# Ten of the convolution's 36 pieces as TensorE products with diagonal matrices, and a new order of all steps

## The chip, the core and the metric

The kernel runs on one core of one Trainium2 chip. The metric is the device time of one execution in microseconds (us), taken as the median of several runs. The core's engines work side by side, each in the order of its own queue: TensorE (PE in the profile, with its weight loads as PEld), VectorE (DVE), ScalarE (ACT), GpSimd (POOL), and SyncE (SP), which here only issues DMA transfers. PE writes PSUM, eight banks of 512 fp32 numbers in each of 128 partitions. ACT and DVE read PSUM; POOL works on SBUF alone.

## The reference

Attention for 8 batches and 8 heads, 576 positions, 64 numbers to a head, then a gated unit over the 512 channels that the heads make together:

```python
scores = scale * np.matmul(q, k.transpose(0, 1, 3, 2))        # scale 1/8
cum = np.cumsum(np.maximum(s, 0.0), axis=-1)
bias = -(cum[:, :, :, None] - cum[:, :, None, :])
scores = np.where(causal, -1000000000.0, scores + np.minimum(bias, 0.0))
attn = softmax(scores)                                        # over the keys
x = np.matmul(attn, v)                                        # (8, 576, 512) after the heads are joined
for k in range(5):
    gate_pre += conv_w[k] * xp[:, k:k + S, :]                 # xp: x with four rows of zeros ahead
out = (sigmoid(gate_pre) * (x @ w_val)) @ w_out
```

The sum over five taps is a causal convolution along the sequence, each channel with its own five weights. It is the part that the change touches.

## The kernel before

A tile is one batch with one pair of heads, which is also one batch with one chunk of 128 channels: 32 tiles, numbered 4 times the batch plus the pair. For each tile the kernel does these steps. The names are those of the table that sets the order; a name is followed by the tile's number.

- `s0 s1 s2` (PE, L508): scores of keys against queries, three groups of two PSUM banks, the two heads side by side in the two halves of PE's rows. `s4` does the last 64 keys of four tiles at once.
- The causal mask on the diagonal blocks: either `mk` (POOL, L585) sets zeros in the exponentials, or, for tiles that have no `mk`, PE adds a product of two constant matrices to the scores (L521), which makes the masked ones hugely negative.
- `e0 e1 e2` (ACT, L563): the exponential, 128x1024 from PSUM into one of the buffers P. `e4` is that of `s4`.
- `av0 av` (PE, L600): exponentials against V, 15 products of 65 columns for each head. V' (`vp`, POOL, L477) is V times a weight from the cumulated s, with a column of twos that gives the sum of the row. `rec nm` (DVE) normalise to half of x.
- `xt` (PE, L632): five transposes bring x to channels by positions, in a PSUM bank. `xe` copies it to SBUF in bf16 (tile xT, L376: all plain copies have this line).
- The convolution, on DVE, POOL and ACT. The taps are divided by the last one, so that this one is the plain x. `t1` (DVE, L671) makes gp = x + ratio * x one position back. `t2 t3 t4` add the other three. On DVE (L676) each is one multiply-add, which reads x in PSUM. On POOL it is two steps: a product `p2 p3 p4` into a buffer pr (L660; a few of the products are done by ACT, L658) and a sum into gp (L679).
- `th` (ACT, L694): tanh of gp times the last tap.
- `val` (PE, L706): x times w_val, four products for each half of 288 positions. `glu` (DVE, L715): (tanh + 1) times it.
- `out` (PE, L726): four products of 512 columns per 128 rows, from the glu tiles of two batches. `oe` copies the result out of PSUM, `st` (SP) stores it.

Around it `ld_q ld_k ld_t ld_v` load (`ld_t`: the last 64 positions of q and k, the tails), `c_q c_k` cast to bf16, `qt` or `qq` transpose q and k on PE, `tt` does that for the tails in fp32 (L483), `qe te` copy the results to QKT (L376). `wu` (PE, L626) is a product of 512 columns that nobody reads; 32 of them stand where PE would have nothing to do. The four tiles of the last batch, 28 to 31, are done in two parts, 384 and 192 positions (`u` and `f` in place of `s` and `e`, and steps named like `t1.29.1`).

The order is a table, ORDER: one entry for each step, with the engine that does it (T is PE, V DVE, A ACT, G POOL, S SP) and the buffers or PSUM banks that it takes. The program reads the table from front to back and gives each engine its steps in that order, and each engine executes its queue strictly in order, waiting at a step until what it needs is there. So the table decides which engine does a step and what stands behind it. BUFS is the number of buffers of each kind: 3 for P, 4 for gp, 2 for pr.

Of the kernel before, what the change touches and what calls it, by code (L numbers as in the profile page):

```python
# [210 lines left out]
t2.3:V ld_t.3:S th.1:A:1 vp.1.2:G wu.31:T:5 av0.4:T:6+7 av.4:T:6+7 e0.5:A:0 rec.4:V vp.1.1:G av0.6:T:4+5 nm.4:V
av.6:T:4+5 e1.5:A:0 s2.5:T:2+3 rec.6:V cast_wv:G s1.7:T:6+7 nm.6:V e2.5:A:0 ld_q.3:S:3 xt.4:T:0 tt.2:T:1 xe.4:V
th.0:A:2 av0.5:T:2+3 t1.4:V:2 c_q.2:G:1 av.5:T:2+3 te.2:A val.3.0:T:4 th.3:A:3 rec.5:V nm.5:V val.3.1:T:1 e1.7:A:2
val.1.0:T:5 glu.3.0:V p4.4:G:1 ld_v.2.2:S xt.5:T:2 glu.3.1:V val.1.1:T:3 c_k.2:A:2 glu.1.0:V ld_v.2.4:S s2.7:T:6+7
glu.1.1:V t4.4:G qq.2.0:T:1:5 xe.5:V val.0.0:T:3 e2.7:A:2 val.0.1:T:4 vp.1.3:G t2.4:V ld_v.2.1:S qe.2.0:A t1.5:V:1
p2.5:G:0 av0.7:T:6+7 glu.0.0:V p3.5:A:1 ld_v.2.3:S glu.0.1:V val.2.0:T:3 t3.4:V qe.2.1:A t2.5:G av.7:T:6+7
qq.2.1:T:4:2 rec.7:V nm.7:V val.2.1:T:0 qe.2.3:A cast_wo:G glu.2.0:V xt.6:T:5 xt.7:T:1 xe.6:V qe.2.2:A s0.9:T:6+7
glu.2.1:V s1.9:T:2+3 ld_v.2.0:S xe.7:V e0.9:A:1 p4.5:G:0 out.0.2:T:0 t1.6:V:0 t1.7:V:3 e1.9:A:1 out.0.0:T:4 ld_k.5:S:4
t3.5:G t4.6:V oe.0.2:A:0 s1.8:T:6+7 s0.8:T:2+3 oe.0.0:A:1 t3.7:V mk.9:G val.7.0:T:0 e0.8:A:0 ld_k.3:S:0 t2.6:V
out.0.3:T:4 p3.6:G:1 e1.8:A:0 t2.7:V out.0.1:T:2 ld_t.4:S t4.7:V th.4:A:4 t3.6:G val.4.0:T:3 val.7.1:T:7 th.7:A:3  # L220
glu.4.0:V st.0.2:S val.4.1:T:1 oe.0.3:V:2 t4.5:G th.6:A:1 s2.8:T:5+6 glu.7.1:V s4.2.3:T:3+4 e2.8:A:0 glu.7.0:V
val.6.0:T:7 glu.4.1:V vp.2.0:G ld_v.3.2:S val.6.1:T:0 glu.6.0:V e4.2.3:A ld_v.3.3:S oe.0.1:V:3 s0.10:T:5+6 th.5:A:2
s2.9:T:3+4 c_q.3:G:0 glu.6.1:V av0.8:T:1+2 e2.9:A:1 av.8:T:1+2 val.5.0:T:0 e0.10:A:2 rec.8:V nm.8:V s2.10:T:3+4
vp.2.1:G val.5.1:T:7 e2.10:A:2 glu.5.0:V s1.10:T:1+2 glu.5.1:V s0.11:T:5+6 ld_q.5:S:1 e1.10:A:2 vp.2.2:G xt.8:T:0
av0.9:T:3+4 xe.8:V tt.3:T:7 e0.11:A:0 t1.8:V:2 p4.8:G:1 av.9:T:3+4 te.3:A qq.3.0:T:1:2 rec.9:V ld_t.5:S nm.9:V
# [5 lines left out]
nm.11:V s0.14:T:3+4 out.0.5:T:7 e0.14:A:2 st.0.3:S oe.0.4:V:3 t2.9:V s4.3.3:T:5+6 ld_v.4.2:S t3.10:G th.8:A:0
xt.11:T:4 ld_v.4.1:S s0.13:T:2+3 e4.3.3:A xe.11:V s2.13:T:0+1 e0.13:A:0 t1.11:V:1 val.8.0:T:5 vp.3.3:G val.10.0:T:6
glu.8.0:V th.10:A:3 t3.11:V s1.13:T:2+3 st.0.4:S vp.3.1:G val.8.1:T:5 e2.13:A:0 glu.10.0:V t2.11:V val.10.1:T:6
e1.13:A:0 mk.13:G val.9.0:T:0 glu.8.1:V oe.0.5:A:5 glu.10.1:V val.9.1:T:1 mk.14:G t4.11:V th.9:A:4 s2.14:T:2+3
qq.5.0:T:7:6 ld_k.6:S:0 e2.14:A:2 glu.9.0:V c_k.5:G:0 av0.13:T:4+5 qe.5.0:V av.13:T:4+5 qe.5.1:A val.11.0:T:0
ld_v.4.4:S rec.13:V glu.9.1:V th.11:A:1 s1.14:T:2+3 s0.15:T:6+7 vp.3.2:G nm.13:V e1.14:A:2 ld_v.4.0:S val.11.1:T:1
glu.11.0:V xt.13:T:4 st.0.5:S glu.11.1:V mk.12:G e0.15:A:0 s1.15:T:2+3 xe.13:V s2.15:T:0+1 t1.13:V:2 e2.15:A:0
c_q.4:G:1 qq.5.1:T:7:6 t2.13:V out.1.1:T:5 qe.5.2:A qe.5.3:V av0.14:T:0+1 e1.15:A:0 c_k.4:G:2 av.14:T:0+1 out.1.2:T:7
p4.13:A:0 rec.14:V nm.14:V oe.1.1:A:2 qq.4.0:T:6:2 oe.1.2:V:3 t4.13:G qq.4.1:T:5:3 qe.4.1:A qe.4.0:V xt.14:T:7
out.1.0:T:0 vp.3.0:G xe.14:A t3.13:V qe.4.2:A av0.15:T:1+2 t1.14:V:0 av.15:T:1+2 p4.14:G:1 ld_v.5.2:S qe.4.3:A  # L240
# [5 lines left out]
th.14:A:0 s0.18:T:6+7 vp.4.3:G rec.16:V e0.18:A:1 val.12.0:T:0 nm.16:V ld_t.6:S th.12:A:3 glu.14.1:V val.12.1:T:6
mk.18:G glu.14.0:V xt.16:T:7 th.13:A:4 oe.1.3:V:4 ld_q.7:S:4 val.15.0:T:3 vp.4.2:G xe.16:A glu.12.1:V s1.18:T:4+5
glu.12.0:V s2.18:T:1+2 e1.18:A:1 val.13.0:T:6 glu.15.0:V st.1.0:S t1.16:V:3 vp.5.2:G val.13.1:T:0 e2.18:A:1 st.0.8:S
s0.19:T:3+4 glu.13.0:V t4.16:V ld_k.7:S:2 s4.5.3:T:5+6 e0.19:A:2 av.18:T:1+2 glu.13.1:V c_q.6:G:1 av0.18:T:1+2 t3.16:V
e4.5.3:A s1.19:T:3+4 rec.18:V s2.19:T:5+6 e1.19:A:2 nm.18:V ld_t.7:S out.1.4:T:0 vp.5.3:G t2.16:V e2.19:A:2 xt.18:T:1  # L250
# [593 lines left out]
```

## Time and profile before

| | |
|---|---|
| timed runs (us) | 188.28, 189.47, 189.51; median 189.47 |
| the profiled execution: its span (us) | 188.0 |
| PE busy (us) | 171.6 (91%), 2724 products |
| DVE busy (us) | 166.1 (88%), 322 instructions |
| ACT busy (us) | 169.2 (90%), 229 instructions |
| POOL busy (us) | 163.7 (87%), 147 instructions |
| granted PE clock, mean | 0.986 |

The profile gives the profiled execution from its first to its last instruction, 188.0 us; the page has no other time of it. That is 0.3 us below the fastest and 1.5 us below the median of the timed runs. Durations of single instructions, as the groups give them, include the time in which an instruction's end runs beside the start of the next one; so a group's busy time divided by its count is what one of them adds to the engine's busy time. For PE the ends are modelled, and what a product really takes of PE is read from one start to the next.

### The profile page before, as it was taken

The numbers are of one execution on the slowest core, as the hardware profiler recorded it, in microseconds if no ns is written. First come the engines' busy times: TensorE is split into PE (matmuls) and PEld (weight loads), VectorE is DVE, ScalarE is ACT, GpSimd is POOL, SyncE is SP. The second block draws the span as 40 slices with busy tenths as digits, with TensorE's granted clock in tenths as the row PEclk, the third lists the DMA queues.
The fourth block names the chain that finished last, engine by engine and source line by source line (L and its number), as shares of the span: only waits on it lengthen the run. The fifth ranks groups of instructions, "written<-read, shape, count | busy, mean of one in ns | idle before, by whom it ended". The sixth has DMA issues, their size and how long they took to land.

```text
span 188.0 us, 6658 instructions
## 1 busy us (share of the span) xinstructions
PE 171.6 (91%) x2724; PEld 113.4 (60%) x2724; DVE 166.1 (88%) x322; ACT 169.2 (90%) x229; POOL 163.7 (87%) x147
## 2 busy tenths in 40 slices
...
GB/s 173 272 279 258 244 222 262 346 386 333 185 251 347 168 307 178 334 331 271 169 257 238 328 389 247 205 307 221 62 59 167 3 2 59 223 5 112 43 202 158
DMA packets 62283, 40.46 MB, mean 215 GB/s; under 512 B 47333, under 2 KB 49381, under 8 KB 62250
## 3 DMA queue, kind: packets, MB, share of 16 engines
...
## 4 chain that ended last, share of the span: by engine, by line
PE 39%; ACT 27%; DVE 17%; issue 7%; DMA 6%; SPq 1%; POOL 1%; ACTq 0%; DVEq 0%
ACT P L563 18%; PE bank L706 11%; PE bank L726 9%; PE bank L600 7%; PE bank L508 6%; ACT QKT L376 4%; DVE gp L676 4%; DMA out_dram<-ot 4%; DVE gp L671 3%; DMA gp<-in_s_dram 3%; ACT th L694 2%; DVE xn L619 2%; PE bank L632 2%; DVE glu L715 2%; PE bank L626 2%
## 5 line engine op out<-in xcount | busy, mean ns | idle before, releaser
L563 ACT ACTIVATE P<-bank 128x1024 bf16<-128x1024 f32 x84 | 83.0, 1046 | 4.2 <-PE bank L508 3.4
L676 DVE SCALAR_TENSOR_TENSOR gp<-bank,cwr,gp 128x573 f32<-128x573 bf16 (+5 forms) x72 | 52.7, 744 | 0.9
L679 POOL TENSOR_TENSOR gp<-gp,pr 128x572 f32<-128x572 f32 (+6 forms) x36 | 45.0, 1255 | 6.6 <-DVE gp L676 4.2
L508 PE MATMUL bank<-QKT 64*128 64x128 bf16 (+4 forms) x592 | 37.4, 238 | 5.0 <-DVE QKT L376 1.8
L477 POOL TENSOR_TENSOR Vp<-vst,w 128x650 bf16<-128x650 f32 x32 | 40.6, 1283 | 1.5 <-DMA qkf<-in_k_dram 1.0
L706 PE MATMUL bank<-xT,wv 128*128 128x288 bf16 (+2 forms) x256 | 37.9, 287 | 1.2 <-ACT P L563 0.4
L600 PE MATMUL bank<-Vp,P 128*128 128x65 bf16 x960 | 35.6, 194 | 2.1 <-ACT P L535 0.9
L600 PEld LDWEIGHTS <-P 128*128 128x128 bf16 x960 | 32.9, 98 | 6.6 <-issue 1.7
L726 PE MATMUL bank<-wo,glu 128*128 128x512 bf16 x144 | 35.6, 380 | 0.3 <-DVE gp L676 0.2
L508 PEld LDWEIGHTS <-QKT 64*128 64x128 bf16 x592 | 19.7, 94 | 23.1 <-issue 15.4
L660 POOL TENSOR_TENSOR pr<-xT,cwr 128x572 f32<-128x572 bf16 (+6 forms) x28 | 28.3, 1017 | 1.3 <-DVE xT L376 1.2
L706 PEld LDWEIGHTS <-wv 128*128 128x128 bf16 x256 | 22.6, 97 | 10.6 <-issue 3.7
L619 DVE TENSOR_TENSOR xn<-bank,recs 128x640 bf16<-128x640 f32 (+2 forms) x36 | 26.9, 748 | 0.9
L715 DVE SCALAR_TENSOR_TENSOR glu<-th,bank 128x288 bf16<-128x288 f32 (+2 forms) x64 | 27.0, 447 | 0.4
L671 DVE SCALAR_TENSOR_TENSOR gp<-xT,cwr,bank 128x576 f32<-128x576 bf16 (+2 forms) x36 | 26.5, 739 | 0.8
L376 ACT COPY QKT<-bank 128x1024 bf16<-128x1024 bf16 (+1 forms) x26 | 24.3, 974 | 2.7 <-PE bank L492 2.4
L585 POOL TENSOR_SCALAR_AFFINE_SELECT P<-P 128x1024 bf16<-128x1024 bf16 (+1 forms) x20 | 20.4, 1027 | 4.1 <-ACT P L563 4.1
L694 ACT ACTIVATE th<-gp,cwr 128x576 f32<-128x576 f32 x28 | 22.1, 802 | 0.2 <-DVE gp L676 0.2
L726 PEld LDWEIGHTS <-glu 128*128 128x128 bf16 x144 | 12.3, 98 | 13.7 <-issue 2.1
L376 ACT COPY ot<-bank 128x512 f32<-128x512 f32 x25 | 14.8, 610 | 2.7 <-PE bank L726 2.0
L632 PE MATMUL bank<-ident,xn 128*128 128x128 bf16 x164 | 14.9, 220 | 0.6 <-ACT P L563 0.3
L376 POOL CAST qkb<-qkf 128x2048 bf16<-128x2048 f32 (+1 forms) x9 | 14.3, 1607 | 0.0
...
## 6 DMA issues: line engine op xcount, KB each, us to landing
...
```

Of the source, the lines that this page charges most:

```text
L376: (act.copy if e is act else e.tensor_copy)(dst, src)
L477: e.tensor_tensor(Vps[b % 2][:, :, HP[p]], vslot(b)[:, :, HP[p]], w[:, :, b * 8 + 2 * p:b * 8 + 2 * p + 2].unsqueeze(3).to_broadcast([128, ...
L508: pe.matmul(ps[:, hh, c0:c0 + nq], QKTs[b % 2][r, 1, p, k0:k0 + 128], QKTs[b % 2][r, 0, p, q0:q0 + nq], **kw)
L563: act.activation(out=Pt(n)[:, :, step * 512:(step + 1) * 512], in_=pair((f"s{step}", n)), func=AF.Exp, scale=0.125)
L600: pe.matmul(ps[:, o:o + 65], lhsT, Vps[b % 2][:, kb, 2 * p + w, :], start=(kb == 0), stop=(kb == qb))
L619: vec.tensor_tensor(xns[b % 2][:, g, p * 128:(p + 1) * 128].rearrange("t g (w d) -> t w g d", w=2), ps[:, :, :, 0:64], recs[:, n, :, g].un ...
L671: vec.scalar_tensor_tensor(gp[:, lo:hi], xT[:, 3 + lo:3 + hi], r, xps(n, *h)[:, lo:hi], ALU.mult, ALU.add)
L676: vec.scalar_tensor_tensor(gp[:, lo:hi], xps(n, *h)[:, lo - m:hi - m], r, gp[:, lo:hi], ALU.mult, ALU.add)
L679: pool.tensor_tensor(gp[:, lo:hi], gp[:, lo:hi], prs[at[f"p{m}", n, *h][0]][:, lo:hi], ALU.add)
L706: pe.matmul(ps, wv[:, dc, c * 128:(c + 1) * 128], xTs[b % 2][:, dc, 4 + lo:4 + hi], start=(dc == 0), stop=(dc == 3))
L715: vec.scalar_tensor_tensor(glu2[:, c, o + lo:o + hi], th[:, lo:hi], 1.0, ps, ALU.add, ALU.mult)
L726: pe.matmul(bank_of(u, i), glu2[:, c, i * 128:i * 128 + 128], wo[:, c, :], start=(c == 0), stop=(c == 3))
```

## The change

1. For ten pieces of the convolution (tiles 1, 2, 7, 10, 15, 20 and 27, the first part of tile 29, the second parts of 28 and 30) the steps `t1` to `t4` and their products are gone. In their place stands `cv` on PE: for each of the five taps, the 128x128 diagonal matrix of that tap's weights is the stationary operand, and xT, shifted by the tap, the moving one; the five products accumulate in PSUM. A whole tile takes two banks and ten products of 288 columns, a part one bank and five products of 384 or 192. `th` then reads PSUM and has no scale, since the taps are not divided here.
2. The diagonal matrices are made at the start, one instruction for each chunk of channels (`dg`, two on DVE, two on POOL): identity times taps. The taps must therefore be there early: `ld_cw` is the first load on SP, and `cwT cwc` follow at once.
3. The order is new from the first entry to the last, and with it who does what. Masks on POOL: 14 `mk` and 4 `ml` (second parts) in place of 18 and 2, and none for tiles 0 to 9. The other 26 convolution pieces use POOL less: 15 sums (36 before) and 15 products (28, and 8 on ACT, before); ACT does none. Three `vp` go from POOL to DVE. Of the copies `qe`, `te`, `xe` ACT gives seven to DVE; POOL takes five more of the casts, four from DVE and one from ACT. 27 `wu` in place of 32. Two loads of the first batch's q are issued by ACT.
4. Buffers: P 4 (3 before), gp 2 (4), ot 5 (6), pr 1 (2).

In the order tables below, a name in front of an arrow is what is written, names behind it are what is read; numbers behind an underscore tell buffers apart. The lines of the changed kernel are some 4 higher (L508 becomes L512, L676 becomes L680, L715 becomes L737); `cv` is L693.

PE at the start, before: the end of the first tile's scores (L508, `s0.0`), then the tails' transposes (L483, `tt.0`), then the next pair's transposes (L492).

```order
L508 LDWEIGHTS QKT_107
L508 MATMUL bank<-QKT_107 128x128
L483 MATMUL bank<-identf,tail_105 128x128 x4
L492 LDWEIGHTS qkb_103
L492 MATMUL bank<-ident,qkb_103 128x128
```

And now, from the last transpose of the first pair (L496) to the first scores (L512):

```order
L496 LDWEIGHTS qkb_102
L496 MATMUL bank<-ident,qkb_102 128x128
L487 MATMUL bank<-identf,tail_105 128x128 x4
L630 LDWEIGHTS ident
L630 MATMUL bank<-ident 128x512
L630 LDWEIGHTS ident
L630 MATMUL bank<-ident 128x512
L512 LDWEIGHTS QKT_107
L512 MATMUL bank<-QKT_107 128x128
```

The tails' transposes and two unread products now stand ahead of the first scores; before, they stood behind them.

PE at tile 7, now: the end of the scores `s2.10`, the first of the five taps of `cv.7`, in its two halves, and the start of the second.

```order
L512 LDWEIGHTS QKT_107
L512 MATMUL bank<-QKT_107 128x192
L693 LDWEIGHTS diags
L693 MATMUL bank<-xT_114,diags 128x288
L693 LDWEIGHTS diags
L693 MATMUL bank<-xT_114,diags 128x288
L693 LDWEIGHTS diags
```

Ten such pairs stand here in one go; behind them come the scores `s1.9`. Before, PE had nothing of the convolution.

DVE at tiles 5 to 7, before: the copy of tile 7's x (L376), then the first step of tiles 6 and 7 (L671; gp_119 is tile 6, gp_122 tile 7) and their further taps (L676), five of six on DVE.

```order
L376 COPY xT_114<-bank 128x576
L671 SCALAR_TENSOR_TENSOR gp_119<-xT_114,cwr,bank 128x576
L671 SCALAR_TENSOR_TENSOR gp_122<-xT_114,cwr,bank 128x576
L676 SCALAR_TENSOR_TENSOR gp_119<-bank,cwr,gp_119 128x572
L676 SCALAR_TENSOR_TENSOR gp_122<-bank,cwr,gp_122 128x573
L676 SCALAR_TENSOR_TENSOR gp_119<-bank,cwr,gp_119 128x574
L676 SCALAR_TENSOR_TENSOR gp_122<-bank,cwr,gp_122 128x574
L676 SCALAR_TENSOR_TENSOR gp_122<-bank,cwr,gp_122 128x572
```

And now: the copies of tiles 5 and 7, then tiles 5 and 6 (gp_121 and gp_120, the only two gp buffers) through their steps.

```order
L375 COPY xT_114<-bank 128x576 x2
L675 SCALAR_TENSOR_TENSOR gp_121<-xT_114,cwr,bank 128x576
L680 SCALAR_TENSOR_TENSOR gp_121<-bank,cwr,gp_121 128x573
L375 COPY ot_129<-bank 128x512
L675 SCALAR_TENSOR_TENSOR gp_120<-xT_114,cwr,bank 128x576
L680 SCALAR_TENSOR_TENSOR gp_120<-bank,cwr,gp_120 128x573
L680 SCALAR_TENSOR_TENSOR gp_121<-bank,cwr,gp_121 128x574
L680 SCALAR_TENSOR_TENSOR gp_120<-bank,cwr,gp_120 128x574
L680 SCALAR_TENSOR_TENSOR gp_120<-bank,cwr,gp_120 128x572
```

Of tile 7 only the copy of its x is left on DVE; that is what `cv.7` on PE reads.

The diff, cut to its core; of the order table the first line of each.

```diff
-BUFS = {'P': 3, 'gp': 4, 'th': 5, 'ot': 6, 'pr': 2, 'qkf': 5, 'qkb': 3}
+BUFS = {'P': 4, 'gp': 2, 'th': 5, 'ot': 5, 'pr': 1, 'qkf': 5, 'qkb': 3}
 ORDER = """
-ld_q.0.0:S ld_k.0.0:A ld_k.0.1:A ld_t.0:S ld_s:S ld_q.0.1:S ld_q.0.2:S ld_k.0.2:S c_k.0.0:V ld_v.0.1:S c_q.0.0:V
...
+wu.3:T:0 wu.4:T:1 ld_cw:S wu.7:T:2 wu.1:T:3 wu.2:T:4 ld_q.0.1:A wu.8:T:5 wu.9:T:6 cwT:T:7 cwc:V ld_k.0.1:S c_q.0.1:G
...
-    sp, cum = gps[2][0:64], gps[3][0:64]
+    sp, cum = ths[3][0:64], ths[4][0:64]
...
+    cwt = one.tile([128, 4, 5], FP32, name="cwt")
+    diags = one.tile([128, 4, 5, 128], BF16, name="diags")
...
     def conv_ratio(e):
         taps = bank[:, at["cwT"][0], 0:20].rearrange("p (c k) -> p c k", c=4)
+        vec.tensor_copy(cwt, taps)
...
+    def conv_diag(e, c):
+        e.tensor_tensor(diags[:, c], ident.unsqueeze(1).to_broadcast([128, 5, 128]),
+                        cwt[:, c, :].unsqueeze(2).to_broadcast([128, 5, 128]), ALU.mult)
...
+    def conv(e, n, *h):
+        b, c = divmod(n, 4)
+        lo, hi = span(*h)
+        cols = [(lo, hi)] if h else [(0, 288), (288, S)]
+        for m in range(5):
+            for j, (a, z) in enumerate(cols):
+                ps = bank[:, at["cv", n, *h][0], 0:z - a] if h else pair(("cv", n))[:, j, 0:z - a]
+                pe.matmul(ps, diags[:, c, 4 - m, :], xTs[b % 2][:, c, 4 + a - m:4 + z - m], start=(m == 0),
+                          stop=(m == 4))
...
     def tanh(e, n, *hf):
+        if ("cv", n, *hf) in at:
+            lo, hi = span(*hf)
+            if hf:
+                act.activation(out=ths[at["th", n, *hf][0]][:, lo:hi], in_=bank[:, at["cv", n, *hf][0], 0:hi - lo],
+                               func=AF.Tanh)
+            else:
+                act.activation(out=thof(n), in_=pair(("cv", n))[:, :, 0:288], func=AF.Tanh)
+            return
```

More of the change, by code (lines that the diff above doesn't have):

```diff
@@ L211 @@
[L211 to L225, printed above, removed]
@@ L231 @@
[L231 to L240, printed above, removed]
@@ L246 @@
[L246 to L250, printed above, removed]
@@ new lines @@
+glu.7.0:V xt.8:T:6 s0.11:T:0+3 xe.8:V t1.8:V:1 ld_k.3:S:4 av.9:T:2+7 mk.10:G e0.11:A:1 val.5.1:T:1 glu.5.1:V
+c_k.3:G:0 s1.10:T:4+5 av0.9:T:2+7 rec.9:V ld_v.3.1:S e1.10:A:0 ld_q.5:S:0 qq.3.0:T:0:3 val.6.1:T:1 nm.9:V
+av0.10:T:4+5 qe.3.1:A c_q.5:G:2 qe.3.0:A glu.6.1:V t4.8:V mk.11:G tt.3:T:2 te.3:A av.10:T:4+5 t2.8:V rec.10:V
+s1.11:T:3+7 e1.11:A:1 nm.10:V st.0.3:S out.0.7:T:1 s2.11:T:0+2 e2.11:A:1 st.0.1:S val.4.0:T:6 glu.4.0:V xt.9:T:3
+xe.9:V p4.9:G:0 oe.0.7:A:3 xt.10:T:7 xe.10:V s0.13:T:4+5 e0.13:A:2 out.0.6:T:6 t1.9:V:0 s0.12:T:0+2 ld_v.3.3:S
@@ new lines @@
+e4.3.3:A t2.11:V s2.14:T:5+7 e2.14:A:0 qq.5.0:T:2:6 t4.11:V qe.5.0:V val.10.0:T:3 th.11:A:2 vp.3.2:G val.9.0:T:0
+av0.13:T:1+4 ld_q.4:S:2 c_k.5:G:1 th.8:A:1 qe.5.1:A glu.10.0:V av.13:T:1+4 rec.13:V s1.14:T:5+7 val.11.0:T:2
+e1.14:A:0 glu.9.0:V val.11.1:T:3 nm.13:V val.8.1:T:0 glu.11.1:V s0.15:T:1+6 ld_k.4:S:3 glu.11.0:V xt.13:T:4
+glu.8.1:V xe.13:V val.8.0:T:3 st.0.8:S s1.15:T:2+5 e0.15:A:1 e1.15:A:1 qq.5.1:T:0:7 s2.15:T:1+6 qe.5.2:A ld_v.4.4:S
+st.0.6:S glu.8.0:V st.0.4:S out.1.1:T:3 e2.15:A:1 oe.1.1:A:2 av.14:T:2+5 t1.13:V:0 qe.5.3:V ld_v.5.4:S av0.14:T:2+5
@@ new lines @@
+s0.18:T:2+4 s1.17:T:1+5 xt.12:T:0 vp.4.1:G xe.15:V cv.15:T:6+7 te.5:V ld_v.5.2:S ld_k.6:S:4 e0.18:A:1 s4.4.3:T:2+3
+xe.12:V val.14.0:T:4 e1.17:A:0 t1.12:V:1 e4.4.3:A th.15:A:3 t2.12:V glu.14.0:V val.15.0:T:1 vp.4.2:G s2.17:T:2+5
+e2.17:A:0 th.13:A:0 t4.12:V ld_q.6:S:0 av.16:T:3+4 t3.12:V th.12:A:2 vp.4.3:G av0.16:T:3+4 val.13.1:T:6 rec.16:V
+val.13.0:T:7 nm.16:V s1.18:T:2+5 e1.18:A:1 val.14.1:T:0 glu.13.1:V glu.15.0:V xt.16:T:3 xe.16:V glu.13.0:V
+s2.18:T:4+6 vp.5.2:G glu.14.1:V out.1.3:T:1 s4.5.3:T:2+5 val.12.1:T:7 t1.16:V:0 e2.18:A:1 oe.1.3:A:0 s1.19:T:0+4
@@ new lines @@
+st.1.8:S out.2.2:T:7 t2.21:V st.1.1:S rec.22:V s0.26:T:0+1 cv.20:T:3+5 e0.26:A:1 ld_v.7.4:S nm.22:V xt.22:T:4
+th.20:A:3 p4.21:G:0 t4.21:G oe.2.2:V:3 vp.6.1:V p3.21:G:0 t3.21:G ld_v.7.2:S vp.7.0:G s1.24:T:2+6 e1.24:A:2
+s0.25:T:0+7 e0.25:A:3 out.2.1:T:1 s2.26:T:3+5 av.23:T:2+6 e2.26:A:1 xe.22:V av0.23:T:2+6 th.21:A:0 out.2.0:T:0
+s2.24:T:3+7 t1.22:V:1 t4.22:V oe.2.1:V:0 s1.25:T:1+5 e2.24:A:2 vp.6.3:G rec.23:V nm.23:V xt.23:T:2 out.2.3:T:6
+t3.22:V s0.24:T:3+4 e1.25:A:3 xe.23:V val.20.0:T:7 oe.2.0:V:4 oe.2.3:A:2 t1.23:V:0 st.1.7:S glu.20.0:V val.21.0:T:0
@@ new lines @@
+t1.25:V:1 p4.25:G:0 s4.7.3:T:0+5 e4.7.3:A u0.30:T:1+3 f0.30:A:3 av.27:T:4+6 av0.27:T:4+6 u1.28:T:0+2 f1.28:A:1
+xt.24:T:5 t2.25:V rec.27:V xe.24:A t3.25:V mk.30:G out.2.4:T:1 oe.2.4:A:1 u0.28:T:0+3 f0.28:A:1 out.2.7:T:2
+oe.2.7:A:3 st.2.7:S nm.27:V t1.24:V:0 u0.29:T:1+7 xt.27:T:4 xe.27:V xt.26:T:6 t4.25:G t4.24:V f0.29:A:2 xe.26:V
+t2.24:V out.2.8:T:0 th.25:A:2 u0.31:T:2+3 f0.31:A:0 st.2.4:S t1.26:V:1 cv.27:T:1+4 p3.24:G:0 st.2.3:S val.27.1:T:7
+oe.2.8:A:0 t3.26:V th.27:A:3 u1.29:T:2+3 t4.26:V glu.27.1:V val.25.0:T:5 mk.28:G f1.29:A:2 t2.26:V u1.30:T:0+1
```

150 lines of the change are left out of this document (76 added, 74 removed).

## Prediction

> **What bounds the kernel now.** First the page: how busy each engine is, and the chain that ended last.
>
> ```profile
> span 188.0 us, 6658 instructions
> PE 171.6 (91%) x2724; PEld 113.4 (60%) x2724; DVE 166.1 (88%) x322; ACT 169.2 (90%) x229; POOL 163.7 (87%) x147
> PE 39%; ACT 27%; DVE 17%; issue 7%; DMA 6%; SPq 1%; POOL 1%; ACTq 0%; DVEq 0%
> ```
>
> Four engines are within 8 us of each other, and the chain passes from one to the next. So I ask by stretches (the windows view; busy us of PE, PEld, DVE, ACT, POOL with counts).
>
> ```profile
> 40.00:146.00 106.00, 101.43 (x1726) 68.76 (x1725) 99.66 (x177) 103.18 (x130) 101.33 (x78) 1.00 0.90 246
> 146.00:183.00 37.00, 36.79 (x506) 24.58 (x502) 34.95 (x81) 33.74 (x58) 30.66 (x34) 1.00 0.22 80
> ```
>
> In the first stretch ACT is fullest (103.2 of 106), in the second PE (36.8 of 37). But a PE product's end runs beside the next product, so its busy time doesn't say what the products need. I take that from starts, in places where PE goes from group to group without a wait (timeline of PE: start, us, line, form, count).
>
> ```profile
> 58.77 0.40 PE L508 MATMUL bank<-QKT 64*128 64x128 bf16 x8
> 59.00 0.38 PE L521 MATMUL bank<-fut,fut 64*128 64x512 bf16 x2
> 59.22 0.38 PE L508 MATMUL bank<-QKT 64*128 64x320 bf16 x4
> 59.53 1.09 PE L600 MATMUL bank<-Vp,P 128*128 128x65 bf16 x30
> ...
> 172.93 1.34 PE L600 MATMUL bank<-Vp,P 128*128 128x65 bf16 x36
> 174.10 0.81 PE L706 MATMUL bank<-xT,wv 128*128 128x384 bf16 x4
> 174.75 0.33 PE L632 MATMUL bank<-ident,xn 128*128 128x128 bf16 x3
> 174.92 0.71 PE L600 MATMUL bank<-Vp,P 128*128 128x65 bf16 x18
> ...
> 177.53 1.89 PE L726 MATMUL bank<-wo,glu 128*128 128x512 bf16 x8
> 179.26 1.48 PE L706 MATMUL bank<-xT,wv 128*128 128x192 bf16 x16
> 180.58 2.75 PE L726 MATMUL bank<-wo,glu 128*128 128x512 bf16 x12
> ```
>
> From one start to the next: 12 score products (8 in 0.23, 4 in 0.31) 0.045 us each; a mask product 0.11; an attention product 1.17 / 36 = 0.0325; 384 columns of val 0.65 / 4 = 0.163; a transpose 0.17 / 3 = 0.057; out 1.73 / 8 = 0.216; 192 columns 1.32 / 16 = 0.0825. The last is 0.43 ns a column, so 288 columns take 0.124. The groups of each stretch (lines view with a window) give the counts.
>
> ```profile
> L706 PE MATMUL bank<-xT,wv 128*128 128x288 bf16 x184 | 27.4, 287 | 1.2 <-ACT P L563 0.4 <-DVE xT L376 0.3 <-DVE glu L715 0.3
> L508 PE MATMUL bank<-QKT 64*128 64x128 bf16 (+4 forms) x348 | 22.4, 239 | 1.1 <-DVE xn L619 0.6 <-ACT QKT L376 0.4
> L726 PE MATMUL bank<-wo,glu 128*128 128x512 bf16 x88 | 22.2, 380 | 0.3 <-DVE gp L676 0.2 <-DVE glu L715 0.2
> L600 PE MATMUL bank<-Vp,P 128*128 128x65 bf16 x570 | 21.0, 194 | 1.2 <-ACT QKT L376 0.9 <-ACT P L563 0.2
> L632 PE MATMUL bank<-ident,xn 128*128 128x128 bf16 x100 | 8.8, 220 | 0.3 <-ACT P L563 0.3
> L635 PE MATMUL bank<-ident,qkb 64*128 64x64 bf16 x384 | 7.6, 190 | 0.6 <-ACT P L563 0.6
> L521 PE MATMUL bank<-fut,fut 64*128 64x512 bf16 (+1 forms) x28 | 4.7, 338 | 0.0
> L483 PE MATMUL bank<-identf,tail 128*128 128x128 f32 x24 | 3.8, 280 | 0.0
> ```
>
> 40 to 146 us: 184 x 0.124 = 22.8, 348 x 0.045 = 15.7, 88 x 0.216 = 19.0, 570 x 0.0325 = 18.5, 100 x 0.057 = 5.7, 28 x 0.11 = 3.1, and the small transposes L635 and L483 at their busy time, 11.4: 96.2 of 106 us, a rate of 0.91.
>
> ```profile
> L726 PE MATMUL bank<-wo,glu 128*128 128x512 bf16 x56 | 13.4, 380 | 0.0
> L706 PE MATMUL bank<-xT,wv 128*128 128x288 bf16 (+2 forms) x72 | 10.5, 286 | 0.0
> L600 PE MATMUL bank<-Vp,P 128*128 128x65 bf16 x216 | 8.6, 194 | 0.0
> L508 PE MATMUL bank<-QKT 64*128 64x128 bf16 (+5 forms) x104 | 5.9, 229 | 0.2 <-DVE glu L715 0.2
> L632 PE MATMUL bank<-ident,xn 128*128 128x128 bf16 x44 | 4.4, 219 | 0.0
> L521 PE MATMUL bank<-fut,fut 64*128 64x384 bf16 (+2 forms) x14 | 2.0, 284 | 0.0
> ```
>
> 146 to 183 us by the same prices: 12.1 + 8.9 + 7.0 + 4.7 + 2.5 + 1.5 = 36.7 of 37, a rate of 0.99. So PE has about 10 us of slack in the middle, none at the end, and 0.99 is what it reaches when all else is ready.
>
> **The change part by part.** What leaves, and the first 40 us (groups of ACT up to 40 us ahead, then those of the whole run):
>
> ```profile
> L658 ACT ACTIVATE pr<-bank,cwr 128x572 f32<-128x572 bf16 (+1 forms) x2 | 1.5, 753 | 0.0
> L376 ACT CAST QKT<-bank 128x512 bf16<-128x512 f32 x2 | 1.2, 598 | 0.0
> L376 ACT CAST qkb<-qkf 128x1024 bf16<-128x1024 f32 x1 | 1.0, 1037 | 0.0
> ...
> L676 DVE SCALAR_TENSOR_TENSOR gp<-bank,cwr,gp 128x573 f32<-128x573 bf16 (+5 forms) x72 | 52.7, 744 | 0.9
> L679 POOL TENSOR_TENSOR gp<-gp,pr 128x572 f32<-128x572 f32 (+6 forms) x36 | 45.0, 1255 | 6.6 <-DVE gp L676 4.2 <-DVE gp L671 1.3
> L671 DVE SCALAR_TENSOR_TENSOR gp<-xT,cwr,bank 128x576 f32<-128x576 bf16 (+2 forms) x36 | 26.5, 739 | 0.8
> L658 ACT ACTIVATE pr<-bank,cwr 128x572 f32<-128x572 bf16 (+3 forms) x8 | 5.8, 719 | 0.3 <-DVE gp L671 0.3
> ```
>
> ACT loses its 8 tap products (5.8) and, net, 8 copies and casts (3 `qe`, 3 `te`, 1 `xe`, 1 cast), which I price like the products, 8 x 0.72 = 5.8: 169.2 becomes 157.6. The tanh of the ten pieces reads PSUM in place of gp; the copies and the products from PSUM are near the same length, so I take nothing. DVE loses 10 first steps (10 x 0.74 = 7.4), 9 further taps (9 x 0.73 = 6.6) and 4 casts (2.9); it gains 7 copies (5.1) and 5 products of 640 or 650 numbers (3 `vp`, 2 `dg`), for which no DVE row stands: between its own 0.73 and POOL's 1.25 each, 3.7 to 6.3, taken at 4.2 since the engine is DVE. 166.1 becomes some 158.5. POOL loses 21 of 36 sums, 21 x 1.25 = 26, and 13 products besides, and bounds nothing any more.
>
> PE gains `cv`: 7 whole pieces of 10 x 0.124 = 1.24, one of 5 x 0.163 = 0.82, two of 5 x 0.0825 = 0.41: 10.3 in all, of it 2.5 (tiles 1 and 2) in the first 40 us. Two groups of 288 columns in place of one of 512 cost nothing here that `val`, which has the same shape, doesn't show. Masks: from tile 8 on one more tile has its mask on PE (+0.22), and the last four tiles have none there (4 x 0.165 and 2 x 0.05 less): -0.5. Seven of tiles 0 to 7 get theirs on PE, +1.5, but inside the first 40 us, where five unread products, the 32 of which only fill gaps, leave. So after 40 us PE's work grows by 7.8 - 0.5 = 7.3, from 132.9 to 140.2.
>
> The Trainium skill (TensorE: Matmul & The Clock Gate, Back-to-back issue gap) gives about 131 ns for a product of 512 columns in a sustained stream; the 0.216 above contradicts it, and by 0.131 PE would keep so much room that only ACT and DVE could bind, which is the first rival below.
>
> The start (timeline of PE and ACT):
>
> ```profile
> 7.07 1.02 ACT L563 ACTIVATE P<-bank 128x1024 bf16<-128x1024 f32 x1 [0.49 <-PE bank L508]
> ...
> 7.20 0.63 PE L483 MATMUL bank<-identf,tail 128*128 128x128 f32 x4 [0.17 <-DMA tail<-in_k_dram]
> ```
>
> The tails' transposes waited for their load until 7.20, with the first exponential already running. Now they stand ahead of the first scores on PE, and their load stands one place later on SP, behind the taps and one of k. So the first scores can't start before 7.2 + 0.63 and two unread products (0.43), 8.3, and the first exponential not before about 8.7: 1.6 later if the load isn't later, 2.6 if it is by 1 us; I take 2.0. Against it, in the first 40 us ACT is rid of 1.5 + 1.2 + 1.0 = 3.7 us of work; what stood at 40 us stands at 38.3.
>
> The wait that is added: `cv` on PE needs the copy `xe` and two free banks; behind it in PE's queue stand scores, for which ACT waits. With 2 gp buffers in place of 4 a `t1` waits for the tanh two tiles before; POOL's sums waited 6.6 us for DVE before, which bounds that at 0 to 6.6; I take 0, since ten pieces need no gp and POOL is off the path. The end keeps its form: after the last product at 183 come a copy, a store and the checks, 4.9 us to 188.0.
>
> The sum: 38.3 + 140.2 / 0.99 + 4.9 = 184.8 us of span. The timed runs before lie 0.3 to 1.5 us over the span; with 0.9, **185.7**.
>
> **The rivals.** *ACT or DVE binds, PE keeps up.* ACT with the idle time of before (18.8) and the later start: 157.6 + 18.8 + 2.0 = 178.4; DVE 158.5 + 21.9 = 180.4: 178 to 183. For it: in the middle stretch ACT is fullest. Against it: PE at a rate of 1 needs 183.4 already, so that the prices would have to be too high. The Trainium skill (Perfetto Trace Analysis, Identifying the Most-Contended Engine) judges PE by its weight loads' busy share, not by its products'; that is 60% here, which speaks for this rival. The stretch from 146 us disagrees: PE doesn't wait there, with PEld at 24.58 of 37.
>
> *No gain.* PE must run at 0.968 to end where it ended before: 140.2 / (188.0 - 38.3 - 4.9). From 0.956 to 0.981 the time stays within 1%. Before, PE reached 0.91 where ACT led; ACT, DVE and POOL now have 7%, 5% and over 20% less to do, so they are ready earlier, which is why I take more.
>
> *Slower.* PE's queue is strict, and each `cv` holds two of eight banks until ACT's tanh, as the scores and attention products do with theirs. If a `cv` or the scores behind it wait for a bank, PE stalls while it is the bound. It decides from a rate below 0.956; at 0.93, 194.0 of span, at the 0.91 of before, 197.3. For it: PE's waits in the middle are already for ACT's P and DVE's xT, which free banks or feed it. Against it: the end stretch, with the same eight banks, has none.
>
> **How the numbers follow.** The forecast (PE at 0.98 or more, span 183 to 186) has 0.42, the first rival 0.14, no gain 0.24, slower 0.20. A measurement of this kernel tells about 1% from no change, so faster is 0.42 + 0.14 = 0.56, the same 0.24, slower 0.20. The range leaves out the lowest of the first rival (below 179) and the worst of the last (over 193, PE below 0.94): 179 to 193.
>
> **What would show it.** In the profile after: ACT near 157, DVE near 159, POOL below 135, ten products of `cv` 1.2 to 1.3 us from the first to the next group's start; the first exponential at 8.7 to 9.7; PE from 40 us to the last product with no wait of over half a us, and its chain share above 39%. Wrong if ACT's or DVE's queue is full to 98% while PE waits (first rival), or if waits of PE before `cv`, or before scores for banks, add up to more than 4 us.

## The result, and the profile after

The changed kernel takes **302.4 us** (median of four; 299.6 to 303.0) against 189.1 us before: 1.594 times as long, 95% interval 1.585 to 1.603. The forecast was 185.7, the range 179 to 193.

The page of the changed kernel, as before: span, busy time by engine, two engines and PE's granted clock in 40 slices, the chain that ended last, and three of the costliest groups. PEclk is the clock that PE was granted, in tenths of full speed.

```profile
span 301.3 us, 6744 instructions
...
PE 211.3 (70%) x2790; PEld 131.1 (44%) x2808; DVE 166.9 (55%) x312; ACT 165.3 (55%) x213; POOL 129.1 (43%) x115
...
DVE  5742526446646574557445636665644535675784
ACT  2464646456854684556446466545744435673853
...
PEclk9975769598999998999769999999997759999998
...
PE 42%; ACT 29%; DVE 18%; issue 5%; DMA 3%; ACTq 1%; SPq 0%; DVEq 0%
...
L567 ACT ACTIVATE P<-bank 128x1024 bf16<-128x1024 f32 x84 | 84.5, 1026 | 84.0 <-PE bank L512 26.9
L512 PE MATMUL bank<-QKT 64*128 64x128 bf16 (+5 forms) x592 | 45.5, 255 | 17.0 <-ACT P L567 9.8
...
L680 DVE SCALAR_TENSOR_TENSOR gp<-bank,cwr,gp 128x574 f32<-128x574 bf16 (+6 forms) x63 | 46.3, 743 | 13.5 <-ACT P L567 10.1
```

Beside PE, which has 84 weight loads more (2808 for 2724), no engine has much more to do than before: ACT 165 us (169), DVE 167 (166), POOL 129 (164), and an exponential still takes 1.03 us. Yet ACT and DVE stand still for nearly half of the span, for a part of every slice from the first to the last. Ahead of the exponentials ACT idled 84.0 us; before, 4.2, as its row on the page of before says:

```profile
L563 ACT ACTIVATE P<-bank 128x1024 bf16<-128x1024 f32 x84 | 83.0, 1046 | 4.2 <-PE bank L508 3.4
```

So the time went into waits, and they are spread evenly, not piled up where `cv` stands. The waits view (engine, what waited, for whom: us in total, times, longest) has kinds of wait that the kernel before had almost none of:

```profile
ACT P L567 <- DVE gp L680: 13.6, 7, 3.7
DVE xT L375 <- ACT P L567: 10.6, 4, 3.4
DVE gp L680 <- ACT P L567: 10.1, 6, 2.2
...
DVE xn L623 <- ACT P L567: 6.0, 4, 2.0
DVE recs L617 <- ACT P L567: 5.8, 4, 1.7
```

An exponential reads scores and writes P; a further tap reads x and writes gp. Neither uses what the other makes. Added up over all such rows, exponentials waited for DVE or DVE for exponentials 89.7 us in this trace, 0.6 us in that of before. The timeline shows one place (start, us, engine, line, what; in brackets the idle time ahead and for whom):

```profile
99.84 1.02 ACT L567 ACTIVATE P<-bank 128x1024 bf16<-128x1024 f32 x1 [1.94 <-DVE recs L617]
...
99.53 0.22 DVE L617 RECIPROCAL recs<-bank 128x10 f32<-128x10 f32 x1 [0.36 <-PE bank L604]
100.90 0.82 DVE L623 TENSOR_TENSOR xn<-bank,recs 128x640 bf16<-128x640 f32 x1 [1.15 <-ACT P L567]
```

The reciprocal and the normalisation are those of tile 9; by the table its attention products lie in banks 2 and 7. The exponential between them, `e1.10`, reads banks 4 and 5. It starts when the reciprocal ends, and the normalisation starts when it has ended. They share no bank, but 4 and 5 lie between 2 and 7.

That points at a line which the change didn't touch. All eight banks are one tensor of the program, `bank`, and every reader of two banks reads them as one strided piece of it:

```python
    def both(two):
        lo, hi = two
        return bank[:, lo:hi + 1:hi - lo, :]
```

Before, the two banks of all 139 pairs are neighbours. In the new table 104 of 146 are not (in the expectations below, 124 of 174, since the attention products of a pair have two entries).

### The profile page after: what moved, and what is told of

Read it like the earlier page. It is cut to its first block, busy times and chain, and to the rows that moved or that the text cites. A ratio compares the mean times of both kernels' runs of the same rounds, so it can differ in the third digit from the quotient of the medians.

```text
span 301.3 us, 6744 instructions
## 1 busy us (share of the span) xinstructions
PE 211.3 (70%) x2790; PEld 131.1 (44%) x2808; DVE 166.9 (55%) x312; ACT 165.3 (55%) x213; POOL 129.1 (43%) x115
## 3 DMA queue, kind: packets, MB, share of 16 engines
q10 hardware_dynamic: 1088, 1.05, 1.1%
## 4 chain that ended last, share of the span: by engine, by line
PE 42%; ACT 29%; DVE 18%; issue 5%; DMA 3%; ACTq 1%; SPq 0%; DVEq 0%
ACT P L567 20%; PE bank L604 9%; PE bank L728 9%; PE bank L512 7%; PE bank L748 7%; DVE gp L680 5%; DVE xn L623 5%; PE bank L693 3%; DVE glu L737 3%; ACT QKT L375 3%; PE bank L636 2%; DVE gp L675 2%; DMA vst<-in_v_dram 2%; ACT P L581 2%; PE bank L487 2%
## 5 line engine op out<-in xcount | busy, mean ns | idle before, releaser
L512 PE MATMUL bank<-QKT 64*128 64x128 bf16 (+5 forms) x592 | 45.5, 255 | 17.0 <-ACT P L567 9.8
L604 PE MATMUL bank<-Vp,P 128*128 128x65 bf16 x960 | 40.9, 202 | 22.0 <-ACT P L567 17.1
L680 DVE SCALAR_TENSOR_TENSOR gp<-bank,cwr,gp 128x574 f32<-128x574 bf16 (+6 forms) x63 | 46.3, 743 | 13.5 <-ACT P L567 10.1
L728 PE MATMUL bank<-xT,wv 128*128 128x288 bf16 (+2 forms) x256 | 43.7, 304 | 10.8 <-ACT P L567 7.1
L589 POOL TENSOR_SCALAR_AFFINE_SELECT P<-P 128x1024 bf16<-128x1024 bf16 (+2 forms) x18 | 16.0, 893 | 64.4 <-ACT P L567 42.1
L512 PEld LDWEIGHTS <-QKT 64*128 64x128 bf16 x592 | 20.0, 98 | 45.8 <-issue 42.5
L737 DVE SCALAR_TENSOR_TENSOR glu<-th,bank 128x288 bf16<-128x288 f32 (+2 forms) x64 | 27.5, 447 | 21.2 <-PE bank L728 13.7
L664 POOL TENSOR_TENSOR pr<-xT,cwr 128x572 f32<-128x572 bf16 (+2 forms) x15 | 17.1, 1140 | 50.8 <-DVE xT L375 35.8
L683 POOL TENSOR_TENSOR gp<-gp,pr 128x572 f32<-128x572 f32 (+2 forms) x15 | 20.9, 1394 | 28.4 <-DVE gp L680 22.2
L617 DVE RECIPROCAL recs<-bank 128x10 f32<-128x10 f32 (+2 forms) x36 | 7.6, 212 | 36.2 <-PE bank L604 20.8
L675 DVE SCALAR_TENSOR_TENSOR gp<-xT,cwr,bank 128x576 f32<-128x576 bf16 (+2 forms) x26 | 19.6, 756 | 6.4 <-ACT P L567 3.4
L748 PEld LDWEIGHTS <-glu 128*128 128x128 bf16 x144 | 12.8, 100 | 22.6 <-issue 10.3
L375 DVE COPY xT<-bank 128x576 bf16<-128x576 bf16 (+2 forms) x25 | 10.9, 442 | 17.1 <-ACT P L567 10.6
```

The lines of the kernel that those rows point to most:

```text
L375: (act.copy if e is act else e.tensor_copy)(dst, src)
L512: pe.matmul(ps[:, hh, c0:c0 + nq], QKTs[b % 2][r, 1, p, k0:k0 + 128], QKTs[b % 2][r, 0, p, q0:q0 + nq], **kw)
L604: pe.matmul(ps[:, o:o + 65], lhsT, Vps[b % 2][:, kb, 2 * p + w, :], start=(kb == 0), stop=(kb == qb))
L675: vec.scalar_tensor_tensor(gp[:, lo:hi], xT[:, 3 + lo:3 + hi], r, xps(n, *h)[:, lo:hi], ALU.mult, ALU.add)
L680: vec.scalar_tensor_tensor(gp[:, lo:hi], xps(n, *h)[:, lo - m:hi - m], r, gp[:, lo:hi], ALU.mult, ALU.add)
L728: pe.matmul(ps, wv[:, dc, c * 128:(c + 1) * 128], xTs[b % 2][:, dc, 4 + lo:4 + hi], start=(dc == 0), stop=(dc == 3))
```

## The experiments

**Theory A: the bank numbers.** A reader of two distant banks is ordered against all users of the banks in between. **Rivals:** B, the order itself (`cv` and masks in PE's queue ahead of scores); C, fewer gp and pr buffers. Four kernels tell them apart. The first gives every pair of the changed kernel neighbouring banks; steps, engines, order and buffers stay (340 entries get other numbers, as here):

```diff
-av.9:T:2+7 ... s1.10:T:4+5 ... s1.11:T:3+7
+av.9:T:2+3 ... s1.10:T:6+7 ... s1.11:T:1+2
```

> Theory A (bank numbers): the changed kernel is slow because the two banks of most of its pairs are not neighbours (124 of 174), and whoever reads such a pair in one instruction is made to wait for the users of the banks in between. With every pair on neighbouring banks, the same steps, engines, order and buffers, the time falls to what the prediction's sum gives, 180 to 192 us; DVE's further taps (L680) no longer wait for ACT (13.6 us and 10.1 us of waits between the two go to under 2). Theory B (the order itself: cv and masks in PE's queue ahead of scores) and theory C (two gp buffers for four, one pr for two): the bank numbers don't matter, the time stays at 285 to 310 us.

Measured: 204.5 us, 1.079 times before (1.076 to 1.082). 98 us are gone, and exponentials and DVE wait for each other 1.0 us. The time is above the 180 to 192 that A expected, which a later run takes up.

The next two are the kernel *before*, with its eight banks renumbered and nothing else:

```diff
-val.5.1:T:7 ... s1.11:T:5+6 ... av.10:T:3+4
+val.5.1:T:4 ... s1.11:T:0+5 ... av.10:T:1+6
```

> The kernel before, with nothing but its eight banks renumbered (0 to 7 become 3 7 2 6 1 5 0 4), so that the two banks of every pair lie 4 or 5 apart. Theory A: far slower, 260 to 340 us, and DVE's taps (L676) and ACT's exponentials (L563) wait for each other, over 20 us in all. Theories B and C: the same steps in the same order with the same buffers, so 188 to 191 us.

> The kernel before, banks renumbered 0 to 7 into 0 2 4 6 7 5 3 1: 123 of 139 pairs lie two apart, with one bank between them, the other 16 are neighbours. Theory A: slower, but less than with three or four banks in between, 215 to 275 us. Theories B and C: 188 to 191 us.

Measured: **351.8 us** with 4 or 5 from bank to bank, **229.2 us** with 2 (one execution each; before ran 188.5 to 190.4 beside them). The first is even above the 340 that A allowed. The page and the waits of the first:

```profile
PE 228.5 (65%) x2724; PEld 142.9 (41%) x2724; DVE 172.2 (49%) x322; ACT 180.7 (52%) x229; POOL 164.9 (47%) x147
...
L556 ACT ACTIVATE P<-bank 128x1024 bf16<-128x1024 f32 x84 | 85.7, 1024 | 106.5 <-PE bank L501 17.2
...
L699 PE MATMUL bank<-xT,wv 128*128 128x288 bf16 (+2 forms) x256 | 47.0, 331 | 14.2 <-ACT P L556 8.6
```

```profile
DVE gp L669 <- ACT P L556: 18.9, 15, 3.3
DVE glu L708 <- ACT P L556: 15.8, 10, 2.9
ACT P L556 <- DVE xn L612: 15.6, 7, 4.3
```

The kernel before, with other bank numbers, shows all of the changed kernel's symptoms. Reading distant banks costs nothing in itself (1024 ns for an exponential; 1046 before): only the waits do. PE's products grow too, 331 ns for one of `val` where L706 had 287, with a mean granted clock of 0.78.

The fourth leaves the changed kernel's banks as they are and splits the readers of distant pairs:

```diff
-            act.activation(out=Pt(n)[:, :, step * 512:(step + 1) * 512], in_=pair((f"s{step}", n)), func=AF.Exp,
-                           scale=0.125)
+            for w, ps in each((f"s{step}", n)):
+                act.activation(out=Pt(n)[:, w, step * 512:(step + 1) * 512], in_=ps, func=AF.Exp, scale=0.125)
```

and the same for the other exponentials, `rec`, `nm` and `cv`'s tanh. `each` gives one bank at a time, unless the two are neighbours.

> The changed kernel with its own bank numbers; where the banks of a pair are not neighbours, the reader (exponential, reciprocal, normalising product, tanh of cv) is split into two instructions, one for each bank. Theory A: the waits go, and what remains is the fixed cost of some 46 more ACT and 32 more DVE instructions (0.16 us each on ACT, by 0.60 us for 512 columns against 1.04 for 1024): ACT 165 becomes 173, the time 186 to 206 us. Theories B and C: more instructions and no relief, 300 to 315 us.

Measured: **194.8 us**, 1.028 times before (1.024 to 1.032). So 107.6 of the 113.3 us came from one way of reading. The 84 instructions more on ACT add little: 166.1 us of work, where 173 was expected. The waits are written into the program and don't arise on the chip: in the trace each instruction carries the semaphores (counters by which one engine tells another that it is done) that it must wait for. The second and third columns count instructions of DVE that carry a wait for ACT, in themselves or in the semaphore instruction right ahead; the fourth adds up the rows of the waits view:

| kernel | further taps that must wait for ACT | normalisations that must | exponentials and DVE waiting for each other (us) | time (us) |
|---|---|---|---|---|
| before | 1 of 72 | 0 of 36 | 0.6 | 189.1 |
| before, distance 2 | 10 of 72 | 1 of 36 | 26.1 | 229.2 |
| before, distance 4 or 5 | 17 of 72 | 11 of 36 | 143.0 | 351.8 |
| changed | 10 of 63 | 6 of 36 | 89.7 | 302.4 |
| changed, neighbours | 0 of 63 | 0 of 36 | 1.0 | 204.5 |
| changed, readers split | 0 of 63 | 0 of 56 | 3.1 | 194.8 |

That readers of one bank on two engines are ordered at all agrees with the Trainium skill (PSUM — Partial Sum Buffer, PSUM bank collisions raise a hardware error), which asks for such a wait between any two engines at the same bank. The trace of before shows one: the product `p4.26` on ACT starts at 153.16, after an idle time put down to DVE, once `t1.26`, which reads the same bank and makes nothing that it uses, has ended at 153.07. With distant banks the wait also stands where no bank is shared.

**What remains.** 194.8 is still 9 us above the forecast. The split kernel's page:

```profile
PE 184.3 (96%) x2808; PEld 117.6 (61%) x2808; DVE 164.8 (85%) x352; ACT 166.1 (86%) x297; POOL 129.8 (67%) x115
...
PE 84%; DMA 5%; ACT 4%; DVE 3%; issue 1%; ACTq 0%; SPq 0%; DVEq 0%
```

and of its windows (busy us of PE, PEld, DVE, ACT, POOL with counts):

```profile
40.00:146.00 106.00, 105.77 (x1778) 69.27 (x1777) 97.69 (x199) 100.72 (x171) 89.66 (x67) 1.00 0.89 250
146.00:188.00 42.00, 42.00 (x555) 27.46 (x554) 37.54 (x93) 34.64 (x72) 15.74 (x17) 1.00 0.21 77
```

PE has 84% of the chain, and from 40 us on it stood still for 0.2 of 148 us. So theory D: PE binds and needs more than the forecast gave it; E: the added instructions on ACT and DVE do it. One kernel renumbers again, with a bank taken again only after its last reader in the split kernel's trace; another leaves four of the five tap products of each `cv` out, so that the gate of these ten pieces has one tap only.

```diff
-            for m in range(5):
+            for m in (4,):
...
-                pe.matmul(ps, diags[:, c, 4 - m, :], xTs[b % 2][:, c, 4 + a - m:4 + z - m], start=(m == 0),
+                pe.matmul(ps, diags[:, c, 4 - m, :], xTs[b % 2][:, c, 4 + a - m:4 + z - m], start=True,
```

> The changed kernel with all pairs on neighbouring banks, as in the run a1_adj (204.5 us), but with numbers chosen so that a bank is taken again only after its last reader in the trace of the split kernel (a3_split, 194.8 us) had ended. Theory D (once the bank waits are gone, PE binds: in the split kernel it stood still nowhere from 40 us on): no split instructions, and no gain from that: 192 to 197 us. Theory E (the split kernel's extra instructions on ACT and DVE cost it the rest, and the forecast's sum was right): 184 to 189 us. If 204 or more, neighbouring banks cost waits however they are numbered.

> The split kernel with four of the five tap products of each cv left out (so the gate of those ten pieces lacks four taps): PE has 68 products less, 7 x 8 x 0.124 + 4 x 0.163 + 8 x 0.0825 = 8.3 us, 6.3 of it after 40 us. Theory D, PE binds: 186 to 189 us. Theory E (ACT and DVE bind): no more than 1 us less than 194.8.

Measured: 195.9 us (1.033 times before, 1.026 to 1.040) without any split instruction: E falls. It also explains the 204.5: that run was not slow because of neighbours, but because of which ones it took; PE stood still for 6.7 of the 148 us after 40 us there, for at most 2.2 here. With one tap 190.4 us (1.008 times, 1.004 to 1.012): 4.4 us less for 6.3 us of products after 40 us. That is far more than E allows, and 1.4 us above D's range: D holds for the larger part, and what is late for the last 2 us wasn't traced. With a fifth of `cv`'s products left the new order is still no faster than the old.

What had the forecast left out of PE's work? The timeline of PE in the split kernel (start, us, line, form, count):

```profile
60.75 0.66 PE L739 MATMUL bank<-xT,wv 128*128 128x288 bf16 x4
61.35 0.40 PE L512 MATMUL bank<-QKT 64*128 64x128 bf16 x8
61.68 0.67 PE L739 MATMUL bank<-xT,wv 128*128 128x288 bf16 x4
...
65.39 0.66 PE L739 MATMUL bank<-xT,wv 128*128 128x288 bf16 x4
65.89 0.61 PE L612 MATMUL bank<-Vp,P 128*128 128x65 bf16 x15
...
71.44 0.40 PE L512 MATMUL bank<-QKT 64*128 64x128 bf16 x8
71.67 0.63 PE L649 MATMUL bank<-ident,qkb 64*128 64x64 bf16 x32
72.23 1.41 PE L703 MATMUL bank<-xT,diags 128*128 128x288 bf16 x10
73.48 1.08 PE L612 MATMUL bank<-Vp,P 128*128 128x65 bf16 x30
```

Four products of `val` take 0.50 us from start to start when others of 128 rows follow (65.39 to 65.89), 0.60 when scores of 64 rows follow (60.75 to 61.35). Eight scores take 0.23 ahead of transposes of 64 rows (71.44), 0.33 ahead of `val` (61.35). So a change of rows costs some 0.1 us each way (theory F). From 40 us on the trace of before has 56 changes from 64 to 128 rows, that of the split kernel 83. Two runs put 56 unread products into it, of 64 rows in one and 128 in the other:

```diff
+                    if not h and i == 2:
+                        pe.matmul(ps[:, 330:394], fut[0][0:64, 0:128], fut[1][0:64, 0:64], start=True, stop=True)
```

```diff
+                    if not h and i == 2:
+                        pe.matmul(ps[:, 330:394], ident, ident[:, 0:64], start=True, stop=True)
```

> The split kernel with one product of 64 rows by 64 columns of two constants put in the middle of the attention products of each head of 28 tiles, 56 in all; nobody reads it. Theory F (a change of PE between products of 64 and of 128 rows costs about 0.1 us on the way in and 0.17 on the way out, as the starts in the trace suggest): 56 x (0.03 + 0.27) = 17 us of PE more, 208 to 213 us. Otherwise 56 x 0.03 = 1.7 us more, 195.5 to 197.5 us.

> The same 56 unread products with 128 rows by 64 columns: no change of rows. Both theories: 56 x 0.03 = 1.7 us of PE more; 195.5 to 197.5 us if PE binds, 194.8 if it doesn't. The difference to the run with 64 rows, over 56, is the price of one change there and back.

Measured: 208.0 (207.6 to 208.7) and 196.6 us (195.8 to 198.1). The difference over 56 is **0.20 us for one change there and back**; the size was expected at 0.27. Eight of the 56 stand before 40 us; if those cost no time, it is 0.24. The Trainium skill (TensorEngine Tiling (Array Packing), Key Properties) says that changing the tiling mode drains TensorE; these runs fit that and put a price on the change, but don't show that it is a drain. At 0.20, 27 changes more are 5.5 us of PE.

Next, the other way: fewer changes, by moving groups of scores next to each other in the kernel with the timed bank numbers.

```diff
-s0.13:T:2+3 ... out.0.6:T:6 ... s0.12:T:4+5
+s0.13:T:2+3 ... s0.12:T:4+5 out.0.6:T:6
```

And the claim that PE had slack before, tested on the kernel before itself:

```diff
+                    if not h and i == 2:
+                        for r in range(3):
+                            pe.matmul(ps[:, 330:458], ident, ident, start=True, stop=True)
```

> The kernel of run a4_timed (195.9 us), in which 17 times a group of scores was moved ahead of the one group of 128-row products (and once of one group of transposes with 64 rows) that stood between it and the scores before it, so that PE changes its rows 15 times less there and back; the same products otherwise. Theory F with the price that the 64-row and 128-row inserts gave, (208.0 - 196.6) / 56 = 0.20 us: 14 to 15 x 0.20 = 3 us less, 192 to 194 us. If the price holds only for inserts: 195 to 197 us.

> The kernel before with 168 unread products of 128 rows by 128 columns in the middle of its attention products (three to a head of 28 tiles), 168 x 0.057 = 9.6 us of PE work, about 7.5 after 40 us, no change of rows. The prediction's reading (PE has some 10 us of slack from 40 to 146 us): 189 to 191.5 us. Theory D (what looked like slack was changes of rows; PE really waits under 5 us there): 193 to 198 us.

Measured: 194.2 us (193.4 to 195.5), 1.7 less than 195.9; the trace has 73 changes after 40 us in place of 84, and the profiled span is 192.5 in place of 194.8. In the right direction and at the edge of what was expected, but the intervals overlap (1.019 to 1.036 times before, against 1.026 to 1.040 with the timed numbers alone), so the size isn't shown. The second is plain: **196.6 us (196.1 to 197.5), 7.4 us more** (some 6.9 of it in the profiled spans), for 7.5 us of products after 40 us. PE's idle time took none of them up: from 40 to 146 us PE is busy 101.78 us, 101.43 before. PE bound the kernel before already, with less than 1 us to spare.

Last the start. The timeline of PE and ACT in the changed kernel:

```profile
9.66 0.40 PE L512 MATMUL bank<-QKT 64*128 64x128 bf16 x8
9.89 0.38 PE L525 MATMUL bank<-fut,fut 64*128 64x512 bf16 x2
...
8.30 0.62 ACT L375 CAST qkb<-first 128x512 bf16<-128x512 f32 x1
12.03 0.43 ACTq L437 DMA_DIRECT2D first<-in_k_dram  x1
12.51 1.02 ACT L567 ACTIVATE P<-bank 128x1024 bf16<-128x1024 f32 x1 [3.59 <-DMA vst<-in_v_dram]
```

The first scores and their mask were done by 10.3, but a load that ACT issues stands ahead of the exponential and waits, by the profile, for an earlier load of v to land. One run moves that issue to SP; another adds masks on POOL to it, to take work off PE.

```diff
-ld_k.0.2:A
+ld_k.0.2:S
```

```diff
+mk.2:G ... mk.3:G ... mk.6:G ... mk.7:G ... mk.5:G ... mk.9:G ... mk.8:G ... mk.14:G ... mk.17:G ... mk.18:G ... mk.20:G ... mk.21:G ... mk.22:G ... mk.25:G
```

Each mask stands right behind its `e0`.

> The kernel of run e1_together (194.2 us), with one entry changed: the third load of k that ACT issues (ld_k.0.2), which stands in ACT's queue ahead of the first exponential and waits there for another load to land (issued at 12.0 us, the exponential at 12.4, though its scores were done by 10.2), goes to SP. Theory G (this wait holds the first exponential back, and the start is late on the path): first exponential at 9.5 to 10.5 us, the time 191 to 193. If the first 40 us aren't on the path: 194 to 195.

> The same with the masks of 14 more tiles as mk on POOL (14 x 0.9 = 12.6 us of POOL, busy 130 us) in place of two products of 512 columns each on PE (28 x 0.11 = 3.1 us of PE, some 2 of it after 40 us). PE binds (theory D): 2 to 3 us less than the run with the load on SP alone, 188 to 191. If POOL's masks come late for the attention products, nothing or slower.

Measured: **192.3 us** (192.2 to 192.5) with the load on SP, 1.9 less than 194.2 (the intervals of the two ratios overlap a little); the first exponential starts at 9.88. With the masks 218.8 us, far from the 188 to 191 that were expected if PE binds: POOL's masks wait for exponentials, 26.4 us (2.8 in the kernel with only the load moved), and PE waits for the casts that are queued behind them.

```profile
POOL P L581 <- ACT P L559: 26.4, 9, 7.7
...
PEld L631 <- POOL qkb L367: 6.8, 3, 3.8
PE bank L631 <- POOL qkb L367: 6.2, 3, 3.7
```

The 3.1 us that PE was spared can't be seen behind that. The best kernel with the change, at 192.3 us, is 1.014 times before (1.007 to 1.022); none beat the kernel before. Rival C was not tried by itself; in the split kernel, which has the changed kernel's buffers, PE waits for nothing after 40 us, so they cost no time there.

## Why the prediction was wrong, point by point

**The step that failed: "The wait that is added".** It looked for a wait of `cv` on two free banks, and for one on gp. The wait that came belongs to the readers of every pair, and stems from the bank numbers, which the prediction never looked at: it read the table for engines and order and took its numbers as free. The sum 38.3 + 140.2 / 0.99 + 4.9 was made for queues that don't wait for each other; in the trace of the changed kernel they do, and PE is busy 77.2 of the 106 us from 40 to 146 (its windows):

```profile
40.00:146.00 106.00, 77.24 (x1160) 49.57 (x1164) 59.38 (x100) 63.72 (x76) 47.24 (x36) 0.92 0.53 146
```

The prediction's own sign came up: PE stood still for 17.0 us ahead of scores, 9.8 of it until an exponential ended, where over 4 was to mean that it is wrong. The sign for it, a chain share of PE above 39%, came true as well (42%) with PE busy for 70% of the span only, so it tells little.

**The rival "slower"** named a shortage of banks and was nearest, at 0.20 and 197. Its mechanism is not what happened: `cv` itself was waited for little (5.6 us by ACT's tanh, and 0.9 ahead of it), and the rival's argument against, that the end stretch has no such wait with the same eight banks, couldn't see that the wait depends on which two of them make a pair.

**"PE has about 10 us of slack in the middle"** is wrong by itself. Its own rows give 1.1 + 1.2 + 0.3 + 1.2 + 0.3 + 0.6 = 4.7 us of idle time there. The rest of the 10 was no slack: changes of rows, which the price list hardly holds, since it was read within groups, are 45 in that stretch by the trace, 45 x 0.20 = 9 us. This account doesn't close. It gives 4 us too many here, and 2 in the end stretch, where the list already fills 36.7 of 37 us and 11 changes come on top; the price of scores, read up to the attention products behind them (59.22 to 59.53), may hold a part of a change. But the rate of 0.99 can't be carried from one stretch to another, and the run with 7.5 us more of PE in the kernel before settles that there was no such slack.

**PE's added work** was right in the products (ten of `cv` take 1.25 us from 72.23 to 73.48; 1.24 was forecast) and lacked the 27 changes of rows, 5.5 us, which the order brings. Without the bank waits the terms are 7.3 + 5.5 - 4.7 of idle time taken up, 8.1 us, and 1.9 for the load in ACT's queue; the two kernels without these waits are 5.4 and 7.0 us slower than the kernel before beside them. Some 3 to 4.6 us on the other side are not traced further; the 3.7 us that ACT was to be rid of in the start are among what could make them.

**The first exponential** was expected at 8.7 to 9.7 and came at 12.51. The step counted the tails on SP and PE, and of the loads on ACT nothing; once that one is gone it is 9.88.

**The sums of the engines.** POOL at 129.1 was right (under 135). ACT without bank waits has 162.0, 4 more than forecast, which wasn't traced further; DVE 165.5 against 158.5. Two groups of DVE in that kernel (the one with timed numbers) show 4.0 of the 7.0 us of the larger miss:

```profile
L472 DVE TENSOR_TENSOR Vp<-vst,w 128x650 bf16<-128x650 f32 x3 | 4.6, 1537 | 0.0
L405 DVE TENSOR_TENSOR diags<-ident,cwt 128x640 bf16<-128x640 bf16 x2 | 3.6, 1814 | 0.0
```

The five products of 640 or 650 numbers were bounded by 3.7 to 6.3 us, POOL's rate as the worse end, and taken at 4.2; they take 8.2. Neither miss can have cost much time, since PE bound. Two smaller terms were off as well. A run's time lies 1.7 to 1.9 us above its own span (2.3 to 2.8 with the 168 products), where 0.9 was taken, from different executions; and DVE's time in the first rival, 180.4, lacks the later start of 2.0 that ACT's has.

**The first rival** (ACT or DVE binds, 178 to 183) never came near: with the bank waits gone PE is at 96%, ACT at 86%. The busy share of the weight loads, 61%, was no measure of what PE could still take.
